# A recurrence and a feed-forward layer on one core: weights kept in SBUF, five inverses by blocks, merged products, a new issue order

## The chip, the core and the metric

The kernel runs on one core of a Trainium2 chip. Its engines each work through a queue of their own, in order: TensorE (PE, with weight loads shown apart as PEld) multiplies from SBUF into PSUM, VectorE (DVE), ScalarE (ACT) and GpSimd (POOL) do elementwise work, and SyncE (SP) does nothing but issue transfers (DMA); GpSimd and ScalarE can issue them too. The metric is the device time of one execution in microseconds. Before the change it is 1139.86 us, the median of three runs (1139.08 to 1140.85).

## The reference, cut to what matters

Two blocks follow each other. The first is a recurrence over 768 time steps for 4 x 8 sequences (batch times heads) with a 40 x 40 state; the second is a gated feed-forward layer over the 3072 tokens of width 320.

```python
for t in range(S):                                   # S = 768
    y[:, :, t] = einsum('bhd,bhde->bhe', rt, state)
    Sa = einsum('bhde,bhe->bhd', state, at)
    state = state * wt[:, :, None, :] - einsum('bhd,bhe->bhde', Sa, bt) \
            + einsum('bhd,bhe->bhde', vt, kt)
x = y as (3072, 320)
xn = x / sqrt(mean(x * x) + 1e-6) * rms_g
g = xn @ w_gate                                      # 320 x 1536
out = (g * sigmoid(g) * (xn @ w_val)) @ w_out        # 1536 x 320
```

The inputs of the recurrence are float32. The feed-forward weights come as float64 in memory, and the kernel makes float32 of them by integer operations.

## The kernel before, in words

Time is cut into 24 chunks of 32 steps (`C = 32`), and all 32 sequences are worked at once: two sequences side by side on partitions 0 to 63 and 64 to 127 in several layouts. Names below are those of the code; the prediction names tiles in the same way.

For each chunk there are three pieces of work.

- `front(c)`: loads w, a (tile `wan`), k, b (`kbn`), v (`VU`) and every second w (`wn`), turns them with TensorE (`turned`), and forms the products of keys with a-vectors level by level, for distances of 4, 8 and 16 steps and, first, for the near diagonal (distances 1 to 3). Each level gives a piece of a 32 x 32 triangular matrix per sequence (`LT`, written through a mask by `where`), decayed keys (`KN`), and decay products (`T`). At its end LT is written to memory (`sB`) and read back with one sequence per partition, four times over (`M`).
- `inverse(c)`: inverts the triangular matrices by substitution, 31 steps of two VectorE instructions (`tmp` and `Yi`), each partition holding a quarter of the rows; the result goes through memory (`sY`) back into the other rows of `LT`.
- `main(c)`: products with the incoming state and LT (`X`), a change of sign (`Xs`), the solve with the inverse (`U`, copied into `VU`), the new state (`ST`), the scores (`sc`, from the turned VU called `vut` and the turned r called `rE`), masked by level into `As`, five products by level and one with the state (`y0`) that make `y`, then the norm and the turned, scaled tile `xg`.

`feed(g)` takes the tokens of two chunks (one, for the first and the last of 13 groups) through the feed-forward layer, in 12 slices of 128 hidden units: 8 matrix products of a slice pair from two tiles `wf`, the gate on ScalarE (`sg`), the product on VectorE (`hT`), and the output product into `po`. Before the first group `narrow` converts each of 24 half slices: it loads raw 64-bit words into a `wf` tile, does five VectorE and three ScalarE instructions, and writes the result to memory (`sW`). Every group then loads each slice of weights from `sW`.

All this is first recorded as pieces with their dependencies and only then issued, in an order that is written out by hand at the top (`ORDER`): each number says which piece comes next, counted from the first piece that is not issued yet. A second list (`PAIRS`) says which of three pairs of PSUM banks a product's room gets. Since each engine takes its queue in order, this list sets what waits behind what. A class `Turns` gives each named tile a fixed number of buffers in rotation (`kbn` three, `LT` three, `KN` three, `T` three, `M` two, `Yi` two, `y` two, `x` two, `wf` five).

A transfer's engine is chosen in `dma`; from chunk 1 on, the loads of w, a, k, b and v are issued by GpSimd, those of r, sB, M, sY, LT, wf and out by SyncE. Line numbers of the profile mostly fall into helpers: L541 is any matrix product, L544 a turn, L495 any VectorE instruction, L522 a ScalarE copy, L538 a transfer.

## Time and profile before

| | us |
|---|---|
| median of three runs | 1139.86 |
| the profiled execution | 1135.55 |
| its span, first to last instruction | 1133.7 |
| TensorE busy | 977.1 (86%) |
| VectorE busy | 874.7 (77%) |
| ScalarE busy | 444.8 (39%) |
| GpSimd busy | 303.2 (27%) |
| moved by transfers | 151.43 MB, 134 GB/s |
| mean granted TensorE clock | 0.953 |

The times of the single parts come from the profiled execution, which is 4.3 us under the median. A float32 product appears in the trace as two instructions with two weight loads, a turn as one. A group's busy time is the time in which at least one of its instructions ran on TensorE, so many small products side by side have a mean far above busy time divided by count. In a group's name, `ps<-Ab,K 40*64 40x56` is a product into a PSUM room from a stationary operand of 40 rows and 64 columns and a moving one of 40 rows and 56 columns. The mean granted clock is the share of full speed that the chip allowed TensorE.

### The profile page before, as it was taken

The page shows a single profiled execution, that of the slowest core. Times are in us where ns is not written, and L with a number is a line of the kernel's source. Part 1 is how long each engine was busy: PE and PEld are TensorE (multiplying, and loading weights), DVE is VectorE, ACT ScalarE, POOL GpSimd, SP SyncE. Part 2 cuts the span into 40 slices and gives each one's busy share as a digit, 9 for nine tenths or more (in the row PEclk, how much of TensorE's full clock was granted, in tenths as well). Part 3 has the DMA queues.
Part 4 walks back from the last instruction along what each step waited for, and adds up shares of the span by engine and source line. Part 5 has one row for each costly group of instructions (what it writes and reads, how often), then busy time and mean ns, then how long its engine had stood idle before and what let it go on. Part 6 is the DMA issues. An engine that isn't in the chain of part 4 may idle for free.

```text
span 1133.7 us, 54781 instructions
## 1 busy us (share of the span) xinstructions
PE 977.1 (86%) x23952; PEld 780.7 (69%) x23952; DVE 874.7 (77%) x3077; ACT 444.8 (39%) x1002; POOL 303.2 (27%) x534
## 2 busy tenths in 40 slices
PE   2426766898999898999899999999899899989998
PEld 2426655776777677777777777776677677767776
DVE  5899979797878668989779699788778769778231
ACT  4654546333424334344334324434334334332311
POOL 8403340413332322331422322420322423100000
PEclk9999786898999899999999899999999899999999
DMA  7754376654545535544544744754453544542435
GB/s 157 210 164 115 82 216 190 182 142 116 133 112 146 122 95 128 153 106 124 130 123 106 171 107 111 191 133 106 115 142 97 131 118 108 150 112 91 124 125 162
DMA packets 172975, 151.43 MB, mean 134 GB/s; under 512 B 123968, under 2 KB 142336, under 8 KB 172736
## 3 DMA queue, kind: packets, MB, share of 16 engines
q1 hardware_dynamic: 154368, 124.96, 39.8%
q0 software_dynamic: 16192, 22.64, 10.1%
q8 instruction: 188, 3.08, 1.1%
q10 hardware_dynamic: 2176, 0.33, 0.2%
q14 instruction: 51, 0.42, 0.1%
HBM read 131.73 MB, written 16.12 MB: 130 GB/s over the span
## 4 chain that ended last, share of the span: by engine, by line
PE 61%; DVE 14%; DMA 11%; issue 6%; SPq 3%; POOL 3%; ACT 1%; DVEq 0%; POOLq 0%; ACTq 0%
PE ps L541 44%; PE po L541 12%; PE ps L544 5%; DMA M<-sB 4%; SPq L538 3%; DVE tmp L495 2%; DVE Yi L495 2%; DMA sB<-LT 2%; DVE y L495 2%; DVE LT L495 1%; DVE ex L495 1%; POOL kbn L538 1%; DVE As L495 1%; DMA sW<-ex 1%; DMA sY<-Yi 1%
## 5 line engine op out<-in xcount | busy, mean ns | idle before, releaser
L541 PE MATMUL ps<-xg,wf 128*128 128x256 f32 (+3 forms) x1872 | 390.8, 396 | 9.7 <-issue 3.9
L541 PEld LDWEIGHTS ps<-xg,wf 128*128 128x128 f32 (+1 forms) x1872 | 284.9, 203 | 67.7 <-issue 22.2
L541 PE MATMUL po<-wf,hT 128*128 128x320 f32 x576 | 187.9, 455 | 3.6 <-DVE hT L495 3.5
L495 DVE TENSOR_TENSOR tmp<-Yi,M 128x60 f32<-128x60 f32 (+24 forms) x744 | 157.0, 211 | 34.8 <-DMA M<-sB 17.9
L495 DVE TENSOR_TENSOR Yi<-Yi,tmp 128x60 f32<-128x60 f32 (+24 forms) x744 | 156.3, 210 | 13.4
L518 ACT ACTIVATE sg<-ps 128x256 f32<-128x256 f32 (+1 forms) x156 | 55.4, 367 | 201.8 <-PE ps L541 197.0
L541 PEld LDWEIGHTS po<-wf,hT 128*128 128x128 f32 x576 | 103.2, 193 | 40.1 <-DVE hT L495 6.3
L541 PE MATMUL ps<-Ab,K 40*64 40x56 f32 x4608 | 91.9, 234 | 39.4 <-DVE Yi L495 15.4
L541 PEld LDWEIGHTS ps<-Ab,K 40*64 40x64 f32 x4608 | 82.6, 147 | 58.3 <-ACT ex L518 13.9
L495 DVE TENSOR_TENSOR hT<-ps,sg 128x256 f32<-128x256 f32 (+1 forms) x156 | 61.4, 399 | 74.7 <-PE ps L541 56.3
L538 POOL DMA_DIRECT2D kbn<-in_k_dram x92 | 53.6, 585 | 207.7 <-PE ps L541 203.7
L538 POOL DMA_DIRECT2D kbn<-in_b_dram x92 | 54.0, 589 | 180.1 <-PE ps L541 178.8
L495 DVE TENSOR_TENSOR K<-K,T 128x512 f32<-128x512 f32 (+1 forms) x192 | 93.0, 490 | 3.4 <-ACT K L522 1.5
L522 ACT COPY KN<-ps 128x640 f32<-128x640 f32 x96 | 66.1, 691 | 73.9 <-DVE LT L495 39.4
L495 DVE TENSOR_TENSOR As<-ps,msi 128x256 f32<-128x256 f32 (+1 forms) x192 | 84.1, 483 | 13.4 <-PE ps L541 13.2
L522 ACT COPY K<-K 128x256 f32<-128x256 f32 (+1 forms) x168 | 72.2, 444 | 51.1 <-PE ps L541 20.7
L538 POOL DMA_DIRECT2D wn<-in_w_dram x92 | 51.8, 565 | 119.1 <-DVE tmp L495 46.9
L541 PEld LDWEIGHTS ps<-As,KN 128*40 128x40 f32 x3072 | 66.0, 126 | 19.6 <-issue 14.8
L541 PE MATMUL ps<-As,KN 128*40 128x32 f32 x3072 | 71.3, 206 | 8.1 <-issue 6.6
L538 POOL DMA_DIRECT2D VU<-in_v_dram x92 | 53.8, 587 | 61.0 <-PE ps L544 35.8
L495 DVE TENSOR_TENSOR y<-y,ps 128x256 f32<-128x256 f32 x119 | 49.8, 419 | 22.8 <-PE ps L541 19.5
L528 POOL TENSOR_TENSOR ss<-ss,mhalf 128x1 f32<-128x1 f32 x24 | 14.6, 610 | 174.4 <-DVE ss L495 174.1
(122 smaller groups left out, 1399.0 us busy)
## 6 DMA issues: line engine op xcount, KB each, us to landing
wf<-sW SPq DMA_DIRECT2D x156, 480.0 KB, 4.4
M<-sB SPq DMA_DIRECT2D x96, 128.0 KB, 3.5
rn<-in_r_dram SPq DMA_DIRECT2D x24, 160.0 KB, 4.4
sW<-ex SPq DMA_DIRECT2D x16, 240.0 KB, 3.1
kbn<-in_b_dram POOLq DMA_DIRECT2D x92, 40.0 KB, 3.5
kbn<-in_k_dram POOLq DMA_DIRECT2D x92, 40.0 KB, 3.3
wan<-in_a_dram POOLq DMA_DIRECT2D x46, 80.0 KB, 3.8
wan<-in_w_dram POOLq DMA_DIRECT2D x46, 80.0 KB, 3.2
```

Of the source, the lines that this page charges most:

```text
L495: plan.add("DVE", time + more + each * size(o), 0.087, lambda at: [fn(at(o), *m(at))], [o], aps(*args))
L518: scalar(o, [a], lambda at: nc.scalar.activation(at(o), at(a), f, **kw), aps(acc), 0.1 if f in (AF.Square, AF.Relu) else 0.0)
L522: scalar(o, [a], lambda at: nc.scalar.copy(at(o), at(a)), extra=more)
L528: plan.add("POOL", 0.5, 0.06, lambda at: nc.gpsimd.tensor_tensor(o, a, b, op), [o], [a, b])
L538: plan.add(by, 0.6 if by == "POOL" else 0.45, 0.0, lambda at: queue.dma_start(out=o, in_=i), [o], [i], load=load, since=since)
L541: return o, lhsT, rhs, lambda at: nc.tensor.matmul(at(o), lhsT, rhs, start=start, stop=stop, skip_group_check=True), 4
L544: return o, i, ident, lambda at: nc.tensor.transpose(at(o), i, ident), 2
```

## The change

It has these parts.

- The 12 slices of feed-forward weights stay in SBUF: `wf` becomes 12 tiles, `narrow` writes its result into them, and the memory tiles `sW`, their writes, and the loads of every group go. Raw words are loaded into slices that are not converted yet; the last slice uses a tile `exs`.
- To make room, other tiles get fewer buffers, and r is loaded into the tile of w and a.
- For the first five chunks (`BLOCKED = 5`) only the two 16 x 16 diagonal blocks of each matrix are inverted, 15 steps on both at once. The block between them is kept (`LB`, copied from PSUM in `front`), and `main` solves twice: with the diagonal inverses, then a product with LB added into X, a change of sign, and the diagonal inverses again.
- The inverse goes into a tile of its own, `LI`, with two sequences' matrices on a diagonal of 64 x 64, so that the solve is 16 products of 64 rows by 64 columns where it was 32 of 32 by 32.
- The scores are 16 products with 128 stationary columns and both halves of r as one moving operand, where they were 32 with 64 columns and one half. Off-diagonal quarters come out too, and the mask drops them.
- The near-diagonal masked copies run over the groups of four in the inner loop (rows of 8 elements), where the inner loop held the 3, 2 or 1 elements of one group.
- Two ScalarE copies of K per level become one.
- ORDER and PAIRS are new.

```diff
-WB = 5
+BLOCKED = 5
...
-    sW = [dram.tile([P, WF], FP32, name=f"sW{f}") for f in range(FT)]
...
-    kbn = Turns(3, [P, N, 2, 64], "kbn", pad)
-    rn = Turns(1, [P, N, 2, 64], "rn", pad)
+    rn = wan
+    kbn = Turns(2, [P, N, 2, 64], "kbn", pad)
...
-    LT_ = Turns(3, [P, NI, C], "LT", whole)
-    KN_ = {l: Turns(3, [P, NI * D], f"KN{l}_") for l in LEVELS[1:] + (32,)}
+    LT_ = Turns(2, [P, NI, C], "LT", whole)
+    LB_ = Turns(2, [P, NI, C], "LB", whole)
+    LI_ = Turns(2, [P, N, 2 * C], "LI", whole)
+    KN_ = {l: Turns(2, [P, NI * D], f"KN{l}_") for l in LEVELS[1:] + (32,)}
...
-    T_ = Turns(3, [P, NI * 63], "T")
+    T_ = Turns(2, [P, NI * 63], "T")
...
-    M_ = Turns(2, [P, C, C], "M")
-    Yi_ = Turns(2, [P, C // 4, C], "Yi")
-    tmp_ = Turns(2, [P, 160], "tmp")
+    M_ = Turns(1, [P, 2, C // 2 * C + C // 2], "M")
+    Yi_ = Turns(1, [P, 2, C // 8 * C + C // 2], "Yi")
+    tmp_ = Turns(2, [P, 80], "tmp")
...
-    y_ = Turns(2, [P, NI, C], "y", whole)
+    y_ = Turns(1, [P, NI, C], "y", whole)
...
-    x_ = Turns(2, [P, DM + 64], "x")
+    x_ = Turns(1, [P, DM + 64], "x")
...
-    wf_ = Turns(WB, [P, WF], "wf")
+    wf_ = [const.tile([P, WF], FP32, name=f"wf{f}") for f in range(FT)]
...
-            where(LT.rearrange("p n (g j) -> p n g j", j=4)[:, :, :, dist:], near[:, dist - 1:dist].rearrange(
-                "p u (g j) -> p u g j", j=4)[:, :, :, dist:].bitcast(U32).to_broadcast((P, NI, 8, m)), g4[:, :, :, at:at + m], more=0.12)
+            where(LT.rearrange("p n (g j) -> p j n g", j=4)[:, dist:], near[:, dist - 1].rearrange(
+                "p (g j) -> p j g", j=4)[:, dist:, None].bitcast(U32).to_broadcast((P, m, NI, 8)),
+                g4.rearrange("p n g j -> p j n g")[:, at:at + m])
...
+            if G == 1 and c < BLOCKED:
+                LB = z["LB"] = LB_.next()
+                copy(LB[:, :, 16:], gr.rearrange("p o n t -> p (o n) t")[:, :, 0:16])
...
-            for x in range(2):
-                copy(side(K1[:, :, x], l, 1), side(K[:, :, x], l, 1))
+            kn_ = lambda k: k.rearrange("p n x (g h l) -> p (n x) g h l", h=2, l=l)[:, :, :, 1]
+            copy(kn_(K1), kn_(K))
...
+        if c < BLOCKED:
+            for i in range(15):
+                n, m = i // 4 + 1, 15 - i
+                tmp = tmp_.next()[:, 0:2 * n * m].rearrange("p (b s t) -> p b s t", b=2, s=n)
+                tt(tmp, Yd[:, :, 0:n, i:i + 1].to_broadcast((P, 2, n, m)), Md[:, :, i:i + 1, i + 1:16].to_broadcast((P, 2, n, m)), MUL)
+                tt(Yd[:, :, 0:n, i + 1:16], Yd[:, :, 0:n, i + 1:16], tmp, SUB)
...
-            dma(LT[rows(i, 1 - q), q::2], sY[seq(i, q)].rearrange("m (s t) -> s m t", s=C), "LT")
+            dma(LI[rows(i, 1 - q), :, (1 - q) * C:(2 - q) * C], sY[seq(i, q)].rearrange("m (s t) -> s m t", s=C), "LT")
...
-        pe("lower", [mm(U[other(i, n), o, col(n % 4)], LT[other(i, n), o * N + slot(n)], Xs[other(i, n), o, col(n % 4)])
-                        for n, i, o in by_q])
+        LI = z["LI"]
+        solve = [mm(U[half(i), o, col(m)], LI[half(i), 4 * o + m], Xs[half(i), o, col(m)]) for m in range(4) for i in range(2) for o in range(2)]
+        pe("solve", solve)
+        if c < BLOCKED:
+            LB = z["LB"]
+            top = lambda r: slice(r.start, r.start + 16)
+            copy(Xs, U[:, :, 0:4 * D])
+            pe("lower", [mm(X[other(i, n), o, col(n % 4)], LB[top(other(i, n)), o * N + slot(n)], Xs[top(other(i, n)), o, col(n % 4)], False, n % 4 == 3)
+                            for n, i, o in by_q])
+            scale(Xs, X[:, :, 0:4 * D], -1.0)
+            pe("solve", solve)
...
-        pe("score", [mm(sc[half(i), o, n, 0:C], vut[part(o), n, half(i)], R["rE"][part(o), n, i, tk])
-                          for n, i, o in each])
+        pe("score", [mm(sc[:, o, n], vut[part(o), n], R["rE"][part(o), n, :, tk]) for n in range(N) for o in range(2)])
+        si = sc.rearrange("p o n (i t) -> p (o n) i t", i=2)
...
-            wfs = [wf_.next() for _ in range(2)]
-            for e, wf in enumerate(wfs):
-                dma(wf, sW[f + e], "wf")
+            wfs = wf_[f:f + 2]
...
-        rw = wf_.next().bitcast(I32).rearrange("p (f w) -> p f w", w=2)[:, 0:n]
+        spare = FT - 1 - f
+        raw = wf_[FT - 1 - (2 * f + h) % min(spare, 4)].bitcast(I32) if spare else exs
+        rw = raw.rearrange("p (f w) -> p f w", w=2)[:, 0:n]
...
-        tt(exf, low, exf, MUL)
-        dma(dst, exf, "sW")
+        tt(dst, low, exf, MUL)
```

## The prediction

> **What bounds the kernel now.** I read the page's busy shares and its 40 slices first, then cut the span where the first feed group ends (its last hidden product is issued at about 222 us), then the groups of the engines in each part, then the waits.
>
> From the page, the shares and the slices:
>
> ```profile
> PE 977.1 (86%) x23952; PEld 780.7 (69%) x23952; DVE 874.7 (77%) x3077; ACT 444.8 (39%) x1002; POOL 303.2 (27%) x534
> ...
> PE   2426766898999898999899999999899899989998
> ...
> DVE  5899979797878668989779699788778769778231
> ...
> PEclk9999786898999899999999899999999899999999
> ```
>
> The busy time of the three stretches (columns: window, length, then busy us with instruction counts of PE, PEld, DVE, ACT, POOL; granted clock, DMA share, GB/s):
>
> ```profile
> 0.00:222.00 222.00, 123.74 (x3520) 108.27 (x3520) 188.35 (x622) 115.65 (x235) 78.30 (x151) 0.89 0.62 163
> 222.00:1090.00 868.00, 814.40 (x20079) 642.56 (x20074) 678.23 (x2433) 322.13 (x747) 224.33 (x382) 0.97 0.49 125
> 1090.00:1133.70 43.70, 38.97 (x364) 29.84 (x362) 8.18 (x24) 7.02 (x22) 0.56 (x1) 0.99 0.47 148
> ```
>
> Two regimes. From 222 us on TensorE is the bound: it is busy 814.40 of 868 us, so all its waits there are 54 us, and nothing that merely frees VectorE, ScalarE or DMA can win more. Before 222 us TensorE is idle for 98 us while VectorE is busy 188 of 222: weight conversion, five fronts and the inverses share one VectorE queue. What the start spends on VectorE is these groups (first 222 us):
>
> ```profile
> L495 DVE TENSOR_TENSOR tmp<-Yi,M 128x60 f32<-128x60 f32 (+24 forms) x120 | 25.2, 210 | 1.8 <-DMA M<-sB 0.8
> L495 DVE TENSOR_TENSOR Yi<-Yi,tmp 128x60 f32<-128x60 f32 (+24 forms) x119 | 24.8, 209 | 1.3
> ...
> L495 DVE COPY_PREDICATED LT<-near,ps 128x384 f32<-128x384 uint32 (+2 forms) x15 | 10.8, 723 | 1.5 <-POOL LT L534 1.5
> ```
>
> The TensorE groups that the change touches, or that resemble what it adds (whole run; busy us, mean ns of one, then idle before them):
>
> ```profile
> L541 PE MATMUL ps<-Ab,K 40*64 40x56 f32 x4608 | 91.9, 234 | 39.4 <-DVE Yi L495 15.4 <-ACT Ab L522 8.5 <-ACT Xs L525 4.8
> ...
> L541 PE MATMUL ps<-rE,vut 40*64 40x32 f32 x1536 | 30.0, 226 | 7.4 <-issue 4.9 <-ACT vut L522 2.0 <-DVE ST L495 0.3
> ...
> L541 PE MATMUL ps<-VU,KN 64*40 64x40 f32 x1536 | 21.6, 213 | 4.2 <-DVE y L495 1.7 <-DVE xg L495 0.9 <-DVE VU L495 0.7
> ...
> L541 PE MATMUL ps<-Xs,LT 32*32 32x40 f32 x1536 | 20.3, 202 | 1.5 <-DMA LT<-sY 0.8 <-DVE LT L495 0.7
> ...
> L544 PE MATMUL ps<-ident,K 40*128 40x40 f32 x384 | 18.3, 245 | 7.4 <-DVE Yi L495 2.4 <-DVE tmp L495 2.0 <-ACT K L522 1.2
> ```
>
> Here busy divided by count is what one costs when its neighbours overlap it. Last, TensorE's largest wait, SyncE's, and the transfers:
>
> ```profile
> PE ps L541 <- issue: 32.0, 24, 2.9
> ```
>
> ```profile
> SPq L538 <- PE po L541: 316.2, 66, 17.1
> ```
>
> ```profile
> wf<-sW SPq DMA_DIRECT2D x156, 480.0 KB, 4.4
> M<-sB SPq DMA_DIRECT2D x96, 128.0 KB, 3.5
> ...
> kbn<-in_b_dram POOLq DMA_DIRECT2D x92, 40.0 KB, 3.5
> kbn<-in_k_dram POOLq DMA_DIRECT2D x92, 40.0 KB, 3.3
> ```
>
> **The change part by part.** I read the new issue order as the old one: each number counts from the first piece not yet issued, so every piece can be named.
>
> *The start (blocked inverses, near copies).* Up to the last VectorE piece of feed group 0 the old order has 592 VectorE pieces, the new one 471, with the same conversions and the same fronts (but for eight pieces of front 5). Inverse pieces fall from 235 (62+62+62+49) to 120 (four chunks of 30). Now they take 25.2 + 24.8 = 50.0 us. The new ones handle 24 to 44 elements; the rows of 28 and 48 elements have 184 and 209 ns, so 195 ns, 23.4 us: 26.6 us less. Near copies: all three forms take 726 ns though they hold 384, 256 and 128 elements, so they pay by rows of three or fewer, 128 rows each. In rows of eight I price them by the masked copy of 256 elements (429 ns): 0.56, 0.43 and 0.29, or 6.4 us in place of 10.8 for the fifteen. The eight front pieces are some 3 us more. Together 34 us of durations. Neighbouring VectorE instructions overlap where they are independent (an inverse piece starts 131 ns after its neighbour then, 255 ns after it where it depends on it), which gives the low end, 18 us; VectorE is idle 15% here, so I stand nearer the upper: **-29 us**. What the blocks add lies beside this: one more ScalarE copy in the front (0.40), two of Xs (0.44 each), 64 more products of 16 rows (0.85 us, the Xs row over 24) and a second solve, 2.3 us in the path of each of five solves. VectorE's queue hides it; without that cover it costs 11 us. Bounds -34 to -10.
>
> *Products.* Solve: 64 instructions a chunk at 20.3/1536 = 13.2 ns become 32 of 64 rows by 64 columns. Nearest rows: VU,KN (64 rows, 40 columns, 14.1 ns) and Ab,K (40 rows, 64 columns, 19.9 ns): 0.45 to 0.64 us against 0.85, I take 0.55, -7 us in 24 chunks. The Trainium skill, "TensorE: Matmul & The Clock Gate", section "LDWEIGHTS (loading the stationary operand)", lets a weight load grow with its columns alone; by it twice the columns at half the count win nothing, and the sum would be 7 us higher. The rows Ab,K and VU,KN go with it only in part: 1.6 times the columns, 1.4 times the cost. Score: 64 at 19.5 ns (1.25 us) become 32 that load 128 columns and stream 64, off-diagonal blocks that the mask then drops. Lower end Ab,K, 0.64 us; upper ident,K, which also loads 40 rows by 128 columns, 47.7 ns, 1.53 us. It is nearest, so +0.28 x 24 = +7. Chunk 4's second solve falls behind the start, +1. Together **+1**, between -23 and +9: the merging itself buys no time that I can see.
>
> *Position.* When the first feed group's last product is issued, the new order is also past chunk 3's solve, y0, turn, score and the first products of group 1, but not three turns: 6.3 against 2.3 us by their rows, **-4** (0 to -4).
>
> *Weights in SBUF.* 156 loads of 480 KB and 24 write-backs leave SyncE (180 of 728 issues). TensorE never waits for wf. SyncE waits 316 us for products to free a wf buffer, with LT, sB and out behind it; yet an inverse ends a median 28 us before the solve that needs it (chunks 5 to 23), so this is hidden. What can win is instruction fetch: the "issue" gaps, 25 us of the 32 after 222 us. The stream loses 128 of some 2,000 TensorE instructions a chunk (6%), and half the traffic that a fetch meets. Bounds 0 and -8, **-4**.
>
> *Merged ScalarE copies* (two of 404 ns to one of 678, three a chunk): ScalarE is 39% busy; nothing, its idle time hides it, and 0.4 us a chunk if not.
>
> *Fewer buffers, tighter order.* kbn, LT, KN and T go from three buffers to two, M, Yi, x and y from two to one, r shares wan's. The k and b loads of chunk c+2 now wait for the last level of chunk c: GpSimd then issues eight at 0.587 us and the last lands 3.4 later, 8.1 us, with wan, wn, VU issues queued behind. The new order puts a median 7.9 us of products (least 6.8, priced by start-to-start steps in gapless stretches) between that level and the turn of kbn: 0.2 us short a chunk. Between solve and the turn of VU it has 0.9 to 1.2 us of products from chunk 5 on, where the old order has a median 4.1; the copies that must lie between took 1.0 us at best (two VectorE copies of 0.48). Short by 0.15. I take **+7**. Bounds 0 and +45: the copies took a median 2.6 us in the old run, because VectorE's queue let them wait; with that wait kept, the new order is short by 45 us in sum over 24 chunks, the old one by 7.
>
> Sum: -29 + 1 - 4 - 4 + 7 = -29. The profiled execution took 1135.55 us (span 1133.7 and 1.85 around it), the median is 1139.86, 4.3 more; the terms lie inside the span, so I set them against the median: **1111 us**.
>
> **The rivals.**
> *The tight order stalls TensorE* (slower). Place: the turn of VU, after each solve. For it: the median 2.6 us above, and a VectorE that is busy 78% after 222 us. Against it: where the old order left about 1 us, as in chunks 19 and 23, the copies were done in 1.0. Price: 38 us more of waits there and 0.5 us a chunk at kbn, 12 in all, so +50 in place of +7, and -36 + 50 = +14: 1154 us. It decides once the new waits pass 36 us, 1.5 us a chunk.
> *The start is not VectorE's.* The chain of waits there alternates DMA of sB and M (5 to 7 us each), products and turns. If these set the pace, and the second solve lies on them, the start gives 10, not 29: 1130 us.
> *Traffic was holding everything.* The mean 134 GB/s falls by more than half. The Trainium skill, "DMA: Bandwidth & Descriptors", section "Latency and other measured facts", says that lighter HBM load shortens the fixed cost of every transfer; no run here shows it yet. As a mechanism of this kernel: M, sB, LT and fetches land sooner, half of the 54 us of TensorE's waits go, and the tighter order costs nothing: -36 - 20 = -56, and 1084 us.
> That the weights' residence does nothing by itself is part of the forecast.
>
> **How the numbers follow.** Forecast 0.41 (1096 to 1126), slow start 0.20, traffic 0.20, stalls 0.19. The range reaches from below the third to within the stalls, 1080 to 1150, leaving out about 0.07 below and 0.10 above. About 0.2% (2.3 us) is what can be told here. Slower: the stalls, 0.19; same: 0.04, out of the slow start's upper end; faster: 0.77.
>
> **What would show it.** First feed group done near 195 us (forecast) or 210 (slow start), with VectorE's inverse pieces there near 23 us; near copies 0.3 to 0.56 us and unequal; score at or above 1.2 us a chunk; "issue" waits under 25 us. TensorE waits on VU copies or kbn above 1.5 us a chunk would make it wrong upward; PE busy over 97% after the start, downward.

## The result, and the profile after

The changed kernel takes 1191.09 us (1188.50 to 1191.98) where the kernel before takes 1139.47 us: a ratio of 1.0451, 95% interval 1.0427 to 1.0476. It is 52 us slower; the forecast was 29 us faster, and the range ended at 1150. The profiled execution took 1190.31 us, its span is 1188.5, so 54.8 more than before. Some executions of one kernel run longer at a lower granted clock; the ratios below leave them out, the medians do not.

The page of the kernel after, shares and slices:

```profile
PE 1041.0 (88%) x22896; PEld 840.1 (71%) x22896; DVE 891.3 (75%) x2917; ACT 445.4 (37%) x945; POOL 304.6 (26%) x534
...
PE   1528788998989899899899899999999999999998
...
DVE  6999867669678777687787787797697686877541
PEclk9998667999998999998989999998899897999799
```

TensorE is busier by 64 us with 1056 instructions fewer, and its clock is granted less (mean 0.929, before 0.953). The three stretches, cut as in the prediction where the first feed group ends (window, length, then busy us with counts of PE, PEld, DVE, ACT, POOL; clock, DMA share, GB/s):

```profile
0.00:226.00 226.00, 149.00 (x3836) 131.71 (x3838) 181.40 (x504) 118.37 (x230) 72.23 (x139) 0.85 0.43 100
226.00:1108.00 882.00, 816.31 (x18112) 647.75 (x18108) 678.05 (x2303) 313.32 (x678) 231.82 (x394) 0.95 0.25 50
1108.00:1188.50 80.50, 75.69 (x962) 60.65 (x958) 31.85 (x111) 13.71 (x38) 0.56 (x1) 0.97 0.10 22
```

The first feed group ends at 225.8 us (before 221.7; forecast 195). From there to the end of the eleventh group it takes 876.7 us (before 832.2), and the rest is 6.3 us longer. So 4 of the 55 us lie in the start, and 44 in the middle, which was to gain.

The groups that answer to those of before, and then the near copies of before:

```profile
L524 PE MATMUL ps<-Ab,K 40*64 40x56 f32 x4608 | 101.8, 251 | 50.3 <-DVE K L478 12.8 <-DVE LT L478 9.7 <-DVE Yi L478 6.7
...
L524 PE MATMUL ps<-rE,vut 40*128 40x64 f32 x768 | 54.0, 295 | 2.1 <-ACT vut L505 1.3 <-issue 0.7
...
L478 DVE COPY_PREDICATED LT<-near,ps 128x384 f32<-128x384 uint32 x24 | 45.2, 1882 | 4.2 <-PE ps L524 4.1
L524 PE MATMUL ps<-Xs,LI 64*64 64x40 f32 x928 | 38.8, 238 | 18.0 <-DMA LI<-sY 12.6 <-issue 2.5 <-ACT Xs L508 2.1
...
L478 DVE COPY_PREDICATED LT<-near,ps 128x256 f32<-128x256 uint32 x24 | 31.0, 1293 | 0.2
L478 DVE COPY_PREDICATED LT<-near,ps 128x128 f32<-128x128 uint32 x24 | 17.3, 719 | 0.2
```

```profile
L495 DVE COPY_PREDICATED LT<-near,ps 128x128 f32<-128x128 uint32 x24 | 17.4, 727 | 0.1
L495 DVE COPY_PREDICATED LT<-near,ps 128x384 f32<-128x384 uint32 x24 | 17.4, 726 | 3.8 <-PE ps L541 2.2 <-POOL LT L534 1.5
L495 DVE COPY_PREDICATED LT<-near,ps 128x256 f32<-128x256 uint32 x24 | 17.4, 726 | 0.1
```

Three things are read here. The scores cost 54.0 us where they cost 30.0, with half the instructions. The solve costs 38.8 (20.3), for 29 solves in place of 24. And the near copies, forecast at 0.56, 0.43 and 0.29 us, take 1.88, 1.29 and 0.72: 93.5 us of VectorE over the run where they took 52.3.

What the last item does to TensorE is seen in one place of the timeline (start us, us, engine, instructions; in brackets the idle time before them):

```profile
332.44 1.15 PE L524 MATMUL ps<-A,K 40*64 40x56 f32 x64
...
333.52 1.99 PE L524 MATMUL ps<-xg,wf 128*128 128x256 f32 x8
333.66 1.88 DVE L478 COPY_PREDICATED LT<-near,ps 128x384 f32<-128x384 uint32 x1
...
335.79 2.06 DVE L478 COPY_PREDICATED LT<-near,ps 128x256 f32<-128x256 uint32 x2
...
337.99 0.70 PE L524 MATMUL ps<-Ab,K 40*64 40x56 f32 x33 [2.47 <-DVE Yi L478]
```

The near copies stand between the product of keys of the near diagonal (`ps<-A,K`) and that of the next level (`ps<-Ab,K`), since VectorE's keys for that level are queued behind them. The order covers this stretch with eight feed-forward products, 2.0 us. The three copies now need 3.9, and TensorE has nothing to do for 2.5 us. Between 226 and 1050 us there are 30 holes ahead of `ps<-Ab,K`, 36.2 us together, 32.9 of them at the first two levels after the near copies; before there were 7 with 3.3 us.

### The profile page after: what moved, and what is told of

The parts are those of the page before. It is cut to its first block, busy times and chain, and to the rows that moved or that the text cites. A ratio compares the mean times of both kernels' runs of the same rounds, so it can differ in the third digit from the quotient of the medians.

```text
span 1188.5 us, 52214 instructions
## 1 busy us (share of the span) xinstructions
PE 1041.0 (88%) x22896; PEld 840.1 (71%) x22896; DVE 891.3 (75%) x2917; ACT 445.4 (37%) x945; POOL 304.6 (26%) x534
## 4 chain that ended last, share of the span: by engine, by line
PE 52%; DVE 28%; DMA 6%; issue 6%; SPq 3%; POOL 2%; ACT 2%; DVEq 0%; ACTq 0%; POOLq 0%
PE ps L524 39%; PE po L524 9%; DVE LT L478 7%; PE ps L527 4%; SPq L521 3%; DVE K L478 3%; DVE y L478 3%; DVE Yi L478 3%; DVE tmp L478 3%; DVE As L478 1%; DVE Ab L478 1%; DVE wf L478 1%; DMA sB<-LT 1%; DMA M<-sB 1%; POOL kbn L521 1%
## 5 line engine op out<-in xcount | busy, mean ns | idle before, releaser
L524 PE MATMUL ps<-xg,wf 64*128 64x256 f32 (+3 forms) x1872 | 391.8, 397 | 6.5 <-DVE LT L478 2.9
L524 PEld LDWEIGHTS ps<-xg,wf 64*128 64x128 f32 (+1 forms) x1872 | 281.7, 201 | 64.6 <-issue 20.7
L478 DVE TENSOR_TENSOR tmp<-Yi,M 128x60 f32<-128x60 f32 (+26 forms) x664 | 138.8, 209 | 38.9 <-ACT Yi L505 15.1
L478 DVE TENSOR_TENSOR Yi<-Yi,tmp 128x60 f32<-128x60 f32 (+26 forms) x664 | 138.0, 208 | 12.9
L524 PE MATMUL ps<-Ab,K 40*64 40x56 f32 x4608 | 101.8, 251 | 50.3 <-DVE K L478 12.8
L524 PEld LDWEIGHTS ps<-Ab,K 40*64 40x64 f32 x4608 | 93.3, 163 | 65.9 <-issue 33.5
L524 PEld LDWEIGHTS po<-wf,hT 128*128 128x128 f32 x576 | 106.9, 198 | 37.3 <-issue 3.8
L478 DVE COPY_PREDICATED LT<-near,ps 128x384 f32<-128x384 uint32 (+2 forms) x72 | 93.5, 1298 | 4.6 <-PE ps L524 4.1
L505 ACT COPY K<-K 128x512 f32<-128x512 f32 x96 | 60.9, 634 | 64.1 <-DVE K L478 33.7
L524 PE MATMUL ps<-As,KN 128*40 128x32 f32 x3072 | 74.9, 209 | 3.8 <-DVE As L478 2.5
```

What stands on the lines that cost most here:

```text
L478: plan.add("DVE", time + more + each * size(o), 0.087, lambda at: [fn(at(o), *m(at))], [o], aps(*args))
L505: scalar(o, [a], lambda at: nc.scalar.copy(at(o), at(a)), extra=more)
L524: return o, lhsT, rhs, lambda at: nc.tensor.matmul(at(o), lhsT, rhs, start=start, stop=stop, skip_group_check=True), 4
```

## The experiments

All ratios are to the kernel before, run on the same chip in the same session; the runs went to several chips, so a difference of two ratios says more than one of two medians. "Base" is the changed kernel with near copies, scores and solve undone (a_all3). The last three columns come from the profiled execution: the end of the first feed group, the time from there to the end of the eleventh, and the summed length of TensorE's clock records of half speed that begin after 226 us. c_micro and c_quad, executed once (1117.58 and 1748.12 us), are read from their traces alone.

| run | median us | ratio (95%) | first group | to the eleventh | half speed |
|---|---|---|---|---|---|
| before | 1139.47 | | 221.7 | 832.2 | 60.8 |
| after | 1191.09 | 1.0451 (1.0427 to 1.0476) | 225.8 | 876.7 | 102.7 |
| a_score | 1157.28 | 1.0204 (1.0103 to 1.0306) | 218.5 | 857.2 | 86.6 |
| a_solve | 1176.65 | 1.0365 (1.0276 to 1.0454) | 219.5 | 880.0 | 139.9 |
| a_near | 1121.80 | 0.9788 (0.9670 to 0.9905) | 209.4 | 812.5 | 20.0 |
| a_all3 | 1091.39 | 0.9610 (0.9543 to 0.9677) | 211.0 | 801.9 | 22.2 |
| c_base | 1098.55 | 0.9773 (0.9654 to 0.9893) | 209.7 | 811.6 | 43.2 |
| c_noblk | 1135.87 | 0.9913 (0.9875 to 0.9952) | 237.2 | 811.4 | 38.7 |
| c_alt | 1109.86 | 0.9698 (0.9649 to 0.9748) | 207.6 | 818.3 | 44.2 |
| c_traf | 1218.02 | 1.0650 (1.0586 to 1.0713) | 225.8 | 892.7 | 137.9 |
| c_trafa | 1171.25 | 1.0418 (1.0268 to 1.0567) | 223.3 | 856.9 | 78.9 |
| c_load | 1290.82 | 1.1363 (1.1266 to 1.1460) | 211.3 | 958.2 | 235.7 |
| b_near | 1171.64 | 1.0272 (1.0145 to 1.0399) | 223.9 | 853.0 | 63.6 |
| b_score | 1149.04 | 1.0129 (1.0026 to 1.0232) | 222.9 | 840.1 | 51.6 |
| b_noload | 1088.30 | 0.9680 (0.9570 to 0.9791) | 219.7 | 788.5 | 16.7 |

### Undoing one part of the change, and all three

a_score, the scores as before:

```diff
-        pe("score", [mm(sc[:, o, n], vut[part(o), n], R["rE"][part(o), n, :, tk]) for n in range(N) for o in range(2)])
+        pe("score", [mm(sc[half(i), o, n, 0:C], vut[part(o), n, half(i)], R["rE"][part(o), n, i, tk])
+                          for n, i, o in each])
```

> The changed kernel with one part undone: the scores are again 32 products of 64 stationary columns with one half of r each. Theory (the merged products cost TensorE, which is the bound): the score group falls from 54.0 to about 30 us busy and the time by about as much, to 1165 to 1172. Rival (the new order and its tight buffers cost the time, products are covered): within 5 us of 1191.

Measured: 34 us less than the changed kernel by the medians, 28 by the ratios (some 12 either way). The group goes from 54.0 back to 28.8 us, 25 us of it; half speed falls too (102.7 to 86.6 us), and what that adds can't be told from noise.

a_solve, 32 products of 32 by 32 again, from the same tile LI:

```diff
-        solve = [mm(U[half(i), o, col(m)], LI[half(i), 4 * o + m], Xs[half(i), o, col(m)]) for m in range(4) for i in range(2) for o in range(2)]
+        solve = [mm(U[other(i, n), o, col(n % 4)], LI[other(i, n), 4 * o + n % 4, (1 - n // 4) * C:(2 - n // 4) * C], Xs[other(i, n), o, col(n % 4)])
+                 for n, i, o in by_q]
```

> The changed kernel with one part undone: the solve is again 32 products of 32 by 32, from the same tile LI. Theory (merged products cost TensorE): the solve group falls from 38.8 us (29 solves) to about 25, and the time by 12 to 16, to 1175 to 1179. Rival (order and buffers): within 5 us of 1191.

Measured: 14 us less by the medians, 10 by the ratios, whose intervals overlap. The group falls by 10.0 us (38.8 to 28.8, the second solves of five chunks included), while the profiled execution had more half speed (139.9 us) and gained only 3. The direct price, 10 us of TensorE's busy time, is shown; what it is worth in the whole time is no larger than the noise.

a_near, the old loop order of the near copies:

```diff
-            where(LT.rearrange("p n (g j) -> p j n g", j=4)[:, dist:], near[:, dist - 1].rearrange(
+            where(LT.rearrange("p n (g j) -> p n g j", j=4)[:, :, :, dist:], near[:, dist - 1:dist].rearrange(
...
```

> The changed kernel with one part undone: the near-diagonal masked copies have rows of 3, 2 and 1 elements again. They took 1882, 1293 and 719 ns in the changed kernel and 726 each before: 93.5 against 52.3 us in sum. Theory (VectorE is the bound only in the first 226 us, where 15 of the 72 run): 8.6 us of it count, 1181 to 1185. Rival (the tighter order made VectorE part of the pace all through; the masked copies into LT hold 7% of the chain of waits): 25 to 41 us less, 1150 to 1166.

Measured: 69 us less by the medians, 76 by the ratios (some 14 either way), far beyond both expectations. VectorE's copies give back 41 us. The profiled execution, the fastest of the four, has a span 84 us shorter: 16 in the start, 64 from there to the end of the eleventh group, 3 behind it. TensorE's holes between 226 and 1050 us fall from 63.4 to 34.8 us in sum, and half speed from 102.7 to 20.0 us. At half speed one us of work costs two (c_quad below: up to 1.7 us for a record of 3.41), so the latter is worth (102.7 - 20.0) / 2 = 41; with the 29 us of holes that makes 70, for the 68 us behind the start. The group that waits shows both, from the page of a_near, idle 16.3 where the changed kernel has 50.3 and busy 91.5 where it has 101.8:

```profile
L524 PE MATMUL ps<-Ab,K 40*64 40x56 f32 x4608 | 91.5, 234 | 16.3 <-DVE K L478 5.4 <-DVE o L478 2.6 <-DVE LT L478 2.5
```

a_all3, the three diffs above together:

> All three undone at once: split scores, split solve, near copies as before. Left of the change are weights in SBUF, blocked inverses, fewer buffers and the new order. Theory (products on TensorE, near copies in the start only): 24 + 14 + 9 less, 1142 to 1148, so that the rest of the change is worth about nothing against 1139.5. Rival 1 (near copies count throughout): 1105 to 1120, the rest of the change is worth 20 to 35 us. Rival 2 (order and buffers cost the time): 1175 or more.

Measured: 1091.39 us, 4% less than the kernel before, and less than any of the three expectations. It beats both kernels; c_base, the same kernel on another chip, does so too (0.9773). So the blocks, the weights in SBUF, the merged copies and the new order together win 26 to 44 us by the two ratios, and three parts of the change lose 77 to 96. The busy line of a_all3, and two groups in their old form (the solve 29 times in place of 24):

```profile
PE 971.0 (89%) x24592; PEld 778.6 (71%) x24592; DVE 849.2 (78%) x2917; ACT 443.2 (41%) x945; POOL 304.2 (28%) x534
...
L524 PE MATMUL ps<-rE,vut 40*64 40x32 f32 x1536 | 29.2, 226 | 1.8 <-ACT vut L505 1.4
L524 PE MATMUL ps<-Xs,LI 32*32 32x40 f32 x1856 | 28.4, 209 | 23.0 <-DMA LI<-sY 15.6 <-issue 3.6 <-ACT Xs L508 2.4
```

### What a masked copy costs

c_micro appends masked copies of 192 elements a partition, in SBUF, to the base (o destination, m mask, d data):

```diff
+            nc.vector.copy_predicated(o[:, 0:192], m[:, 0:192], d[:, 0:192])
+            nc.vector.copy_predicated(o[:, 0:768:4], m[:, 0:192], d[:, 0:192])
+            nc.vector.copy_predicated(o[:, 0:192], m[:, 0:768:4], d[:, 0:192])
+            nc.vector.copy_predicated(o[:, 0:192], m[:, 0:192], d[:, 0:768:4])
+            nc.vector.copy_predicated(o[:, 0:768:4], m[:, 0:768:4], d[:, 0:768:4])
...
```

> Base: the kernel with the three undone parts, with 32 masked copies and 4 plain copies of 192 elements a partition added behind its last piece, all in SBUF, on lines 1047 to 1054 and 1056: all contiguous; destination alone with a step of four elements; mask alone; source alone; all three; runs of three; runs of three in the destination alone; runs of two (128 elements). Theory (every contiguous run costs 4.5 ns above some 140 ns, whichever operand is cut up): contiguous 0.33 us, the four with a step of four 1.0 us, runs of three or two 0.43 us. Rival 1 (the destination alone counts): mask alone and source alone 0.33 us. Rival 2 (it was the source in PSUM that cost): all near 0.33 us. The time is some 15-25 us above 1091.

Measured, lines in the order of the diff, then runs of three in all operands, runs of three in the destination alone, runs of two, and a plain copy with a step of four on both sides (duration in ns: least, median, most):

```profile
L1047 DVE COPY_PREDICATED wf<-wf,wf x4: 364/374/375, 1093.4 to 1108.4; 128x192 f32<-128x192 uint32 x4
L1048 DVE COPY_PREDICATED wf<-wf,wf x4: 1007/1007/1012, 1093.8 to 1108.8; 128x192 f32<-128x192 uint32 x4
L1049 DVE COPY_PREDICATED wf<-wf,wf x4: 493/494/498, 1094.8 to 1109.8; 128x192 f32<-128x192 uint32 x4
L1050 DVE COPY_PREDICATED wf<-wf,wf x4: 501/506/507, 1095.3 to 1110.3; 128x192 f32<-128x192 uint32 x4
L1051 DVE COPY_PREDICATED wf<-wf,wf x4: 1010/1012/1012, 1095.9 to 1110.9; 128x192 f32<-128x192 uint32 x4
L1052 DVE COPY_PREDICATED wf<-wf,wf x4: 443/444/444, 1096.9 to 1111.9; 128x192 f32<-128x192 uint32 x4
L1053 DVE COPY_PREDICATED wf<-wf,wf x4: 442/444/445, 1097.4 to 1112.4; 128x192 f32<-128x192 uint32 x4
L1054 DVE COPY_PREDICATED wf<-wf,wf x4: 443/444/444, 1097.9 to 1112.9; 128x128 f32<-128x128 uint32 x4
L1056 DVE COPY wf<-wf x4: 335/336/336, 1113.4 to 1114.5; 128x192 f32<-128x192 f32 x4
```

A cut-up destination alone costs as much as all three operands cut up; a cut-up mask or source adds 0.12 to 0.13 us. Runs of two or three cost the same, 444 ns for 64 runs. So the first rival holds in the main: the pieces of the destination set the price. 1007 less 444 ns for 192 less 64 pieces is 4.4 ns a piece. The near copies fit: 128, 256 and 384 pieces took 719, 1293 and 1882 ns, 4.5 ns more for each. In the old form every copy had 128 pieces, of three, two or one element, and all took 726 ns. A plain copy with the same step takes 336 ns: this is a property of the masked copy.

b_near, the kernel before with the new near copies alone:

```diff
-            where(LT.rearrange("p n (g j) -> p n g j", j=4)[:, :, :, dist:], near[:, dist - 1:dist].rearrange(
+            where(LT.rearrange("p n (g j) -> p j n g", j=4)[:, dist:], near[:, dist - 1].rearrange(
...
```

> Base: the kernel before. The near-diagonal masked copies alone take the new form (groups of four in the inner loop); all else, the order too, is as before. Theory (each destination run costs, so 93.5 us of VectorE in place of 52.3, and VectorE's lateness turns into TensorE gaps that also lower the clock): 41 us or more, ratio 1.035-1.065, half-speed time after 226 us above the 61 us of before. Rival (the old order, with more products between, hides most of it): at most 15 us, ratio below 1.013.

Measured: a ratio of 1.0272, some 31 us. The rival (15 us) is below; the theory's 41 is inside the interval (17 to 46), but its reason is not borne out whole. The holes above 1 us grow from 33.9 to 47.9 us, and half speed stays where it was (63.6 against 60.8 us). The old order gives the copies more cover: behind 226 us it has a median 5.5 us of products between `ps<-A,K` and the next `ps<-Ab,K`. The new one has 1.9 to 3.6 us in 11 of its 19 chunks there, and in the other 8 none before the first level; the same edit cost 69 to 76 us in it.

### What the merged products cost

b_score, the kernel before with the merged scores alone:

```diff
-        pe("score", [mm(sc[half(i), o, n, 0:C], vut[part(o), n, half(i)], R["rE"][part(o), n, i, tk])
-                          for n, i, o in each])
+        pe("score", [mm(sc[:, o, n], vut[part(o), n], R["rE"][part(o), n, :, tk]) for n in range(N) for o in range(2)])
```

> Base: the kernel before. The scores alone take the new form (16 products with 128 stationary columns and both halves of r). Theory (the dense step is 1.85 in place of 1.065 us a chunk, and TensorE is the bound): 0.785 x 24 = 19 us, a few more through the clock, ratio 1.014-1.025. Rival (the forecast's price): 7 us, ratio 1.006.

Measured: 1.0129, some 15 us, interval 3 to 26, which holds both prices. The group settles the price of the products, 51.7 us in place of 30.0:

```profile
L541 PE MATMUL ps<-rE,vut 40*128 40x64 f32 x768 | 51.7, 288 | 2.3 <-ACT vut L522 2.2
```

c_alt, the merged solve back in the base, even and odd sequence pairs in turn:

```diff
-        solve = [mm(U[half(i), o, col(m)], LI[half(i), 4 * o + m], Xs[half(i), o, col(m)]) for m in range(4) for i in range(2) for o in range(2)]
+        solve = [mm(U[half(i), o, col(m)], LI[half(i), 4 * o + m], Xs[half(i), o, col(m)]) for m in range(4) for o in range(2) for i in range(2)]
```

> Base: the kernel with the three undone parts (1091.4 us). The merged solve of 16 products of 64 rows by 64 columns is put back, but its products are issued so that neighbours go to different quadrants of TensorE (even, odd sequence pair in turn) instead of four instructions in a row to the same one. Theory (the merged solve was slow because neighbours shared a quadrant): the solve's dense step falls from 1.13 us a chunk to 0.55-0.65 us, below the split form's 0.72; time 1086-1092. Rival (a product of 64 by 64 costs what it costs in any order): dense step 1.1 us, time 1100-1106.

Measured: the time from the solve's first product to the next piece's first, where nothing waits, is 1.149 us a chunk (1.134 in the changed kernel, 0.720 split). The order of the products changes nothing, so the theory of neighbours in one quadrant fell for runs of four instructions (c_quad below has 128 in a row). The time lies between the two measurements of the base and tells nothing more.

c_quad, products measured by themselves behind the base, 64 of each kind (A stationary, X moving):

```diff
+        for n in range(64):
+            prod(p[0:64, 0, 0:40], A[0:64, 0:64], X[0:64, 0:40])
+        for n in range(64):
+            prod(p[half(n % 2), n % 2, 0:40], A[half(n % 2), 0:64], X[half(n % 2), 0:40])
+        for n in range(64):
+            prod(p[half(n // 2 % 2), n % 2, 0:40], A[half(n % 2), 0:64], X[half(n % 2), 0:40])
...
```

> Base: the kernel with the three undone parts; behind its last piece follow, on SBUF data that nobody needs, 64 products each of six kinds: 64 rows by 64 columns in one quadrant of the array; the same in the two diagonal quadrants in turn; the same in all four; 32 by 32 in the four diagonal 32-blocks; 40 rows by 128 columns with 64 moving columns; 40 by 64 with 32 moving columns in all four quadrants. Theory (a product keeps its tile of the array busy for a time of its own, and only different tiles run side by side): 70, 35, 17, 11, 58 and 17 ns an instruction, two instructions a product. Rival (35 ns whatever the tile): the first three alike. Then 30 blocks of 41 dense products, after each of which TensorE waits for a chain of VectorE steps, five times each for 1, 2, 3, 4, 6 and 8 steps of about 0.33 us. Theory (a gap of more than about 1 us costs half speed in the stretch that follows it): no half-speed record behind the shortest gaps, one of 3.4 us or more behind most gaps over 1.5 us. Rival (the half-speed stretches have another cause, power or the mix of products): as many behind short gaps as behind long ones, or none.

Measured, a window for each kind in the order of the expectation (window, length, PE busy with instructions, granted clock):

```profile
1098.00:1108.70 10.70, 10.70 (x133) 0.67 0.06 17
1108.70:1115.40 6.70, 6.70 (x133) 0.50 0.01 2
1115.40:1119.00 3.60, 3.60 (x143) 0.55 0.02 5
1119.00:1121.10 2.10, 1.51 (x130) 1.00 0.00 0
1121.10:1130.90 9.80, 9.80 (x132) 0.72 0.01 3
1130.90:1134.40 3.50, 3.50 (x129) 0.50 0.02 5
```

The clock was half in much of this, so length times clock, over 128 instructions, is the price at full clock: 56, 26, 15, 16, 55 and 14 ns. One quadrant, two, four: 56, 26, 15. A product occupies its own tile of the array and only different tiles run side by side. Hence the two merged forms: the scores' 32 instructions of 128 columns at 55 ns (1.8 us a chunk; 1.85 in the kernel) against 64 in four quadrants at 14 (0.9; 1.07 in the kernel), and a solve that uses the two diagonal quadrants only and leaves the two others idle. The solve's 35 ns an instruction in the kernel is more than the 26 here, and the split solve's 11 less than 16; the kind of the effect is shown, its size here is not the kernel's.

One thing here has nothing to do with holes. From 1098.0 to 1118.7 us TensorE is busy without a break, and yet the 17.1 us from 1101.6 on are at half speed: with these small products the clock fell although nothing was waited for.

The second half of c_quad: 41 dense products of 128 rows (18.0 us at full clock), then a wait of TensorE for a VectorE chain, 29 times.

| hole, us | blocks | half speed behind it | next block |
|---|---|---|---|
| 0.52 | 5 | 0 | 17.97 |
| 0.98 | 5 | 0 | 17.97 |
| 1.43 | 5 | 0 | 17.96 |
| 1.89 | 5 | 1 | 19.65 with, 17.96 without |
| 2.81 | 5 | 3 | 19.34 to 20.99 with, 17.96 without |
| 3.73 | 4 | 3 | 19.65 with, 17.97 without |

The theory holds for these dense products with another threshold: not about 1 us, but near 2, and then by chance. A record of half speed is 3.41 us long (one of 6.83), begins within 1.2 us of the next block's start, and costs 1.4 to 1.7 us (the long one 3.0).

### The start

c_noblk, full inverses in the first five chunks:

```diff
-BLOCKED = 5
+BLOCKED = 0
```

with the pieces of each inverse spread over the places of its blocked form in the order.

> Base: the kernel with the three undone parts (1091.4 us). The first five inverses are full again (31 steps, no blocks, no second solve); each blocked inverse's 30 VectorE pieces become the 62 (49 in the fifth) of the old order, in the same place of the order. Theory of the forecast (the start is VectorE's: 26.6 us of pieces go): the first feed group ends 20-29 us later, at 231-240 us, time 1111-1120. Rival (the chain of transfers and products sets the start): up to 10 us later, time at most 1102.

Measured: the first feed group ends 26.2 us later (237.2 against 211.0), as the theory has it, and the time is 16 to 35 us above the two measurements of the base. The start is VectorE's; the rival falls.

### The weights' traffic

c_traf adds, beside each pair of slices, two copies of 480 KB from memory (`i`) to memory (`o`) on SyncE's queue:

```diff
+                nc.sync.dma_start(out=o, in_=i)
```

> Base: the kernel with the three undone parts (1091.4 us). SyncE issues, beside every pair of feed-forward slices, two extra copies of 480 KB from memory to memory, 156 in all, as many and as large as the weight loads that the change removed; nothing reads them. Theory (traffic was hidden; weights in SBUF win at most the instruction fetch): time 1089-1097, TensorE's issue waits up from about 15 us toward 25. Rival (traffic was holding the kernel): landing of M and k, b back to 3.3-3.5 us, issue waits back to 32 us, time 1105-1115.

Measured: 1.0650, 100 to 119 us above the base. Both expectations are far off. TensorE's waits, of c_traf:

```profile
PE ps L525 <- DMA LI<-sY: 47.2, 22, 8.9
PE ps L525 <- issue: 21.5, 23, 3.0
```

The base waits 15.6 us for LI. The copies read and write memory, more than the loads did, and share SyncE's queue, so this bounds the loads' price from above only.

c_load, loads of 480 KB into one unused SBUF tile in place of the copies, from the second group on:

```diff
+                nc.sync.dma_start(out=exs, in_=i)
```

> Base: the kernel with the three undone parts (ratio to before 0.961). From the second feed-forward group on, SyncE issues two extra loads of 480 KB beside every pair of slices, into one SBUF tile that nobody reads (144 in all, the place and size of the weight loads that the change removed; no memory-to-memory copies). Theory (what made the copies cost 119 us was that other transfers on the same rings, sB, M, sY and LI, landed later, and the new order leaves little room there): landing of M and LI again 3.4-4 us and 3 us, TensorE's waits for LI above 30 us, time 30-70 us above the base, ratio 0.99-1.02. Rival (the copies cost because they also write memory, 87 MB; loads alone are hidden, as the forecast had it): within 10 us of the base, ratio at most 0.97.

Measured: 1.1363. This run answers another question. SyncE's own waits, of c_load:

```profile
SPq L533 <- DMA exs<-in_moe_w_gate_dram: 337.3, 100, 5.4
```

Each load into the same tile waits for the one before it, and everything behind it in SyncE's queue waits too. It is a stalled queue, not traffic, and says nothing on the loads' price.

c_trafa, the copies of c_traf from ScalarE's queue:

```diff
-                nc.sync.dma_start(out=o, in_=i)
+                nc.scalar.dma_start(out=o, in_=i)
```

> Base: the kernel with the three undone parts. The same 156 extra copies of 480 KB from memory to memory as before, but issued from ScalarE's queue, so that SyncE's transfers (sB, M, sY, LI, out) don't stand behind them in one ring. Theory (the 119 us came from standing behind a copy): landing of sB, sY and LI back to 2.1-2.4 us, waits for LI back under 20 us, time within 30 us of the base. Rival (traffic as such: engines and memory are shared whichever queue issues): landings as with SyncE's copies (2.8, 2.7, 3.1 us), time 80-125 us above the base.

Measured on one chip with c_base: 73 us above it, so above the theory's bound and just below the rival's. The waits for LI fall to 8.0 us, yet the time stays high: standing behind a copy is a part of c_traf's cost, not most of it. What ScalarE pays to issue them is in the 73 us.

b_noload, the kernel before without its loads of weights from the third group on:

```diff
-                dma(wf, sW[f + e], "wf")
+                dma(wf, sW[f + e], "wf" if g < 2 else "none")
```

> Base: the kernel before, its order unchanged. From the third feed-forward group on the loads of weights are left out (132 of 156), so these groups multiply by stale weights and the output of their tokens is not the reference's; the products are as many and as large. Theory (the forecast's -4 us holds in the old order, whose cover hides the loads; the 30 us of the middle come from the order and need it): 1-8 us faster, ratio 0.993-0.999, issue waits down from 32 toward 20 us. Rival (traffic held the old kernel too): 20-35 us faster, ratio 0.970-0.983, TensorE gaps after 226 us down from 53 to about 42 us and half-speed time from 61 to about 22 us.

Measured: 1088.30 us, a ratio of 0.968, 36 us less by the ratio (24 to 49) and 45 by the spans, which are single executions of different sessions. The rival holds, somewhat above its range: the loads held the old kernel too. TensorE's waits from 222 to 1090 us, of the kernel before:

```profile
PE ps L541 <- issue: 25.0, 19, 2.9
PE ps L541 <- DVE y L495: 6.0, 3, 3.6
PE ps L544 <- DVE Yi L495: 3.3, 3, 2.4
```

and of b_noload:

```profile
PE ps L541 <- issue: 17.5, 19, 1.9
PE ps L544 <- DVE hT L495: 2.3, 2, 1.8
PE ps L544 <- issue: 1.3, 3, 0.8
```

The same 19 issue waits are shorter, and the single waits on VectorE of 2 to 4 us are gone. TensorE's holes between 226 and 1050 us go from 53.3 to 25.9 us, half speed from 60.8 to 16.7. That is 27 us and 22 us, for 44 us between the first and the eleventh group. The transfers land sooner: M 3.0 us (3.5), k and b 2.6 to 2.7 (3.3 to 3.5), LT 2.3 (3.1). But the edit also takes away SyncE's wait for a free wf buffer (316 us for `po` before, 31 here), behind which sB, LT and out stood. Which of the two closed the holes was not separated; that k and b, which GpSimd issues, land sooner too speaks for the traffic.

c_base, the base once more, with no further edit:

> The kernel with the three undone parts once more, beside the two others on one chip: ratio to before 0.955-0.968, as measured; a ratio outside says that chips differ by as much as the smaller effects here.

Measured: 0.9773, above the expected bracket. The two measurements of one kernel are 1.6% apart, so differences of that size between kernels that ran on different chips (c_alt against the base) are not told from nothing.

## Why the prediction was wrong, point by point

The account in spans: the kernel before 1133.7; without the loads 1088.9 (-44.8); the base 1094.1 (+5.2: start -8.7, middle +13.4, tail +0.5); the changed kernel 1188.5 (+94.4). These are single executions of different sessions, so parts of a few us are within the noise; on one chip c_base's median is 10 us above that of b_noload.

**The start (-29 forecast).** Half right. "Inverse pieces ... 23.4 us": measured 22.8, and c_noblk shows that they are worth 26.2 us on the path. The near copies failed: "in rows of eight I price them by the masked copy of 256 elements" took the loop's inner extent for the unit, where it is the contiguous piece of the destination, and the new form makes every element a piece. (The 429 ns belong to copies in pieces of 4, 8 and 16 elements, 64 pieces at most.) The row that could have told it was in the same list: 384, 256 and 128 elements at one price of 726 ns, 128 pieces each, was read as "rows" there, and rightly; what wasn't asked is whether a row of eight elements, four apart, is still one piece. That moved the first group's end by 9 to 16 us (a_near 209.4; after 225.8, and 218.5 and 219.5 in a_score and a_solve, which keep the new copies). The third miss: without blocks the new order's first group ends at 237.2, 15.5 us later than the old one's. VectorE has 6 us more to do before that point (eight more instructions of the scores' mask, two of VU, and others). Another 8 are overlap: its durations there add up to 237.9 us (before 231.8) and it is busy for 202.0 (188.0), so neighbours overlap by 35.8 us in place of 43.8; 7.5 of the 8 are lost at the inverse pieces. The last 1.5 are idle time. In the base too neighbours overlap by 34.9 us only: its durations are 24 us shorter than before, and with 9 us of overlap lost and 4.5 us more of idle time the first group ends 11 us sooner. The prediction had named the overlap as its low end, 18 us, and stood nearer the upper.

**The near copies were counted in the start alone.** This is the largest error. 57 of the 72 copies lie behind 222 us, where the prediction had TensorE as the bound and gave VectorE's work no price. But a slower VectorE is not the same as a faster one: the chain keys - near copies - keys - products had 2 us of cover at the place shown, and the copies now need 3.9. Undone, they give back 69 to 76 us, the start included: most of what the three parts lose. It is the slow-side rival's kind of mechanism (a tight order that stalls TensorE), at another place.

**Products (+1).** The signs of the terms were: solve -7, scores +7. Measured: solve +10 (groups of a_solve), scores +22 to 25. The scores' upper bound, "ident,K, 47.7 ns, 1.53 us", was too low; 1.85 is 58 ns an instruction. The old form's 1.25 us was too high, 1.07 where nothing waits. The solve's rows, VU,KN and Ab,K, came from products that spread over all four quadrants, and a busy time divided by count carries this overlap along. The merged solve uses two. The Trainium skill, "TensorE: Matmul & The Clock Gate", section "Part 3: Packing small matmuls — row/col tiling", says that a weight load overlaps with products in flight only when they are in other row groups; c_quad's step from 56 to 26 ns, where neighbours go to other row groups, agrees; the step from 26 to 15, where the rows alternate as before and the columns change too, is not in that rule. The rule on weight loads that the prediction weighed (columns alone) gave 0 for the solve; the measurement is worse than either.

**Position (-4).** Not seen by itself; it lies in the 15.5 us above.

**Weights in SBUF (-4, bounds 0 and -8).** Failed by a factor of ten: b_noload gives -36 (24 to 49) for 132 of the 156 loads. The step that failed is "TensorE never waits for wf ... so this is hidden". A transfer that nobody waits for still delays others. The third rival named traffic and half of the 54 us of waits, 27 us (its sum takes 20), and 27 is what the holes lost; it left out the clock, another 22. That rival's citation of the Trainium skill, "DMA: Bandwidth & Descriptors", section "Latency and other measured facts" (lighter load on memory, smaller fixed cost of a transfer), agrees with M at 3.0 in place of 3.5 us and LT at 2.3 in place of 3.1; whether the memory's load or that of the transfer engines (49% busy, then 27%) did it is open. "What can win is instruction fetch" stays unshown: the issue waits fell from 25.0 to 17.5 us, and no run ties them to fetches.

**Merged ScalarE copies (0).** Not tested by itself; ScalarE is 37% busy, and nothing contradicts it.

**Fewer buffers, tighter order (+7, bounds 0 and +45).** In range, at another place. The base's middle is 13 us longer than b_noload's (c_base's 23). The turn of VU, the named place, costs TensorE 2.1 us of waits between 222 and 1090 us in the base and k and b almost none; the wait is at the solve, for LI:

```profile
PE ps L524 <- issue: 11.1, 12, 1.9
PE ps L524 <- DMA LI<-sY: 5.9, 8, 1.6
```

Before, the corresponding line is 0.2 us. Whether the order or the single buffers of M and Yi make LI late was not separated.

**The signs to look for.** Issue waits after 226 us fell to 14.6 us and scores were above 1.2 us a chunk, as named; the first feed group was done at 225.8 us, not near 195. Near copies are unequal as forecast, and three times as long. The waits that were to make it wrong upward, on VU copies and kbn, are not where it went wrong.

## What to carry to other kernels

Price an instruction by what its addresses look like, not by its loop extents, and price a small product by the tiles that its neighbours occupy: a mean of overlapping products does not transfer to a shape that overlaps less. Where the path engine is covered by a fixed amount of work, ask of every other engine's slowdown whether it exceeds that cover; the gain of a faster helper may be nothing there, but the loss of a slower one isn't. And take transfers that nobody waits for away once, by experiment, before writing that they are hidden.

## What the runs showed of the hardware that I had not expected

- A masked copy on VectorE pays 4.4 to 4.5 ns for each contiguous piece of its destination, whether it holds one, two or three elements; a mask or source with a step of four elements adds 0.6 to 0.7 ns an element (494 and 506 against 374 ns for 192). A plain copy of the same step pays none of it (336 ns).
- Holes in TensorE's stream can cost twice. In otherwise dense work no hole up to 1.4 us (15 tried) was followed by half speed, one of five at 1.9 us and six of nine at 2.8 to 3.7 us were, each for 3.41 us or twice that. The Trainium skill, "TensorE: Matmul & The Clock Gate", section "Part 1: The HAM clock gate (the "warmup" mystery)", describes a free-running window of some 3.4 us and two states, full and half; the records' lengths and the chance character agree. Its section "HAM oscillation — how this bites in real kernels" gives the rule as no gaps above about 3.4 us; here holes of 1.9 and 2.8 us were enough. In the changed kernel, whose work is less dense, 14 of the 17 half-speed stretches between 226 and 1100 us have a hole of 1.2 to 2.4 us in the 6.8 us ahead of them, and three have none above 0.8; 6.8 us taken anywhere in that stretch hold such a hole one time in five. That the 102.7 us of half speed there come from the holes is argued from this and from a_near, where both fell together.
- Holes are not the only way to half speed: in c_quad small products without a break ran 17.1 us at it. Nor do longer holes always bring more of it: in b_near they grew by 14 us and half speed by 3. What part of the 102.7 us comes from the kind of product was not separated.
- Between 222 and 1050 us the loads of weights are the difference between 125 and 60 GB/s, and between transfer engines 49% and 27% busy. Without them the others landed 0.5 to 0.8 us sooner, and the time fell by 36 us (24 to 49) in a kernel in which TensorE's products wait for none of them.
